# A reordered prologue: state 1 behind the second Wo piece, and five filler matmuls

## The chip, the cores and the metric

One core of one Trainium2 chip runs the kernel. The metric is the device time of one execution in microseconds (us); the median of a few runs is taken.

## The reference

There are eight batches, `x` of 8 heads x 512 x 64 and `state` of 8 heads x 32 x 64 each.

```python
def _attn_ref(x, state):
    scores = scale * x @ state^T            # softmax over the 32 states
    xread = softmax(scores) @ state         # 512 rows a head
    sread = softmax(scale * state @ x^T) @ x   # 32 rows a head
    return concatenate([xread, sread], axis=2)
def _moe_ref(x, w1, w2, w_out):             # x: 4352 tokens x 512 (8 heads x 64)
    return maximum(x @ w1, x @ w2) @ w_out  # d_ff = 1024
```

## The kernel before

The kernel folds weights together so that the large products are few. max(a, b) is written as relu(a - b) + b: `wd` = W1 - W2 (`w_sub`, L433), and W2 times Wo is folded into one 512 x 512 matrix `wwo` (`ww_mm`, L441, which reads W2 transposed by `w2_mm`, L423, and the cast Wo). For each batch `sw_mm` (L323) multiplies the batch's states by `wd` and `wwo`; `l1_mm` (L353) multiplies that by the transposed softmax `aT` and gives the hidden layer, whose relu goes to `r`; `l2_f` (L368) multiplies `r` by Wo and `l2_open` (L363) adds the `wwo` part. Batches 2 to 7 run in a loop (L550). Batches 0 and 1 run together with all the loading and preparing of weights, in a prologue whose order is written out by hand.

That order is the string `ORDER` (from L18). Each token is one step, and `step` issues the steps in sequence; each engine keeps its own in-order queue, so the order of the tokens is the order in every queue:

- A token without `:` or `>` is a DMA on SP's queue: `ldx.b.g` half of batch b's x, `ldw1.q` and `ldw2.q` a 512 KB piece of W1 or W2, `ldwo.f0.f1` a 512 KB piece of Wo, `ldS.lo.hi` the states of batches lo to hi-1, `xtd`, `atd` and `std` transposes, `store` an output.
- A token with `:` is TensorE work into the PSUM banks behind the colon: `S` transposes states (L181), `xt` x (L222), `at` the softmax (L277), `sc` the scores (L239), `sr` the state reads (L289), `w2` (L423), `ww.i.f0.f1` a part of wwo's row block i (L441), `swh.b.z` and `sw.b.4` eight row-tiled matmuls of `sw_mm` (64 rows x 32 columns of the array each, L323), `l1.b.f` two matmuls (L353), `l2p` and `l2o` parts of the second layer, `idle.n.w` n matmuls of zeros with w columns (L448), whose result nobody reads.
- A token with `>` is an eviction, a cast or other elementwise work on ScalarE (`>A`), VectorE (`>V`) or GpSimd (`>P`): `cS.lo.hi` casts states, `ce` and `cb` cast x, `cw2` and `cwo` cast weights, `sub.q.k` subtracts, `red` sums the softmax, `nm` normalises it.

State 1 means batch 1's state, 64 KB. Its steps are `ldS.1.2` (load), `cS.1.2` (cast), `S.1.2` (two transposes), `S.1.2.0` and `S.1.2.1` (two evictions), and from there `swh.1.0`, the first product with it. The second Wo piece is `ldwo.2.4`; VectorE casts it in `cwo.1`, and the first readers are `ww.3.2.4`, `ww.2.2.4` and their like. A step that writes a bank waits until what was in the bank is evicted.

Of the kernel before, what the change touches and what calls it, by code (L numbers as in the profile page):

```python
# [15 lines left out]


ORDER = """  # L18
ldx.0.1 ldx.0.0 ldw2.1 ldwo.0.2 ldS.1.2 ldw2.0 ldw1.0 ldw1.1 ldwo.2.4 ldx.1.1 ldw2.3 ldw2.2 ldwo.4.6 ldwo.6.8
ldw1.2 ldw1.3 ldx.1.0 ldx.2.1 ldx.2.0 ldS.2.8 idle.9.512:7 cS.0.1>V ce.0.2>V S.0.1:0 S.0.1.0>A ce.0.3>P xt.0.2:1  # L20
S.0.1.1>A xt.0.2>V xt.0.3:7 ce.0.0>V ce.0.1>A xt.0.3>V xt.0.0:3 xt.0.1:4 xt.0.0>A sc.0.1:5 xt.0.1>V sc.0.1>A
sc.0.0:6 cw2.1>V sc.0.0>A red.0.1>V w2.1:2 sr.0:0 w2.1>A cwo.0>P red.0.0>V cS.1.2>A sr.0>V nm.0.1>P ww.2.0.2:1
cw2.0>A S.1.2:7 ww.3.0.2:3 nm.0.0>V S.1.2.0>A w2.0:4 S.1.2.1>A sub.0.0>V at.0.0:5 w2.0>A at.0.1:6 sub.0.1>V
sub.1.1>V at.0.0>A ww.1.0.2:2 ww.0.0.2:0 at.0.1>A sub.1.0>V cwo.1>V swh.0.0:7,4 swh.1.0:5,6 swh.0.0.1>A swh.0.0.0>V
ww.1.2.4:2 swh.1.0.1>A ww.0.2.4:0 swh.1.0.0>V l1.0.0:4 l1.0.3:7 l1.0.0>A l1.0.2:6 ce.1.2>V l1.0.1:5 ce.1.3>P
l1.0.3>V l1.0.2>A xt.1.2:4 ww.2.2.4:1 l1.0.1>A xt.1.2>V cw2.3>P xt.1.3:7 ww.3.2.4:3 xt.1.3>V l2p.0.1.0.2:6 w2.3:4
cw2.2>P sc.1.1:5 w2.3>V l2p.0.3.0.2:7 sc.1.1>A l2p.0.3.2.4:7 red.1.1>V w2.2:4 l2p.0.1.2.4:6 w2.2>A l2p.0.0.0.2:5
cwo.2>V l2p.0.0.2.4:5 nm.1.1>V cwo.3>A ww.2.4.6:1 ww.0.4.6:0 ww.3.4.6:3 sub.2.1>V ww.3.6.8:3 sub.2.0>V ww.0.6.8:0
ww.3>A ww.2.6.8:1 sub.3.1>V ww.0>A ww.1.4.6:2 ww.1.6.8:2 sub.3.0>V ww.2>A l2p.0.2.0.2:4 ww.1>A ce.1.0>V swh.0.1:3,0
ce.1.1>P l2p.0.2.2.4:4 swh.0.1.1>A swh.0.1.0>V xt.1.0:1 xt.1.1:2 xt.1.0>A l1.0.5:0 xt.1.1>V cb.2.1>P l1.0.4:3  # L30
l1.0.5>A sc.1.0:1 l1.0.4>V l1.0.6:2 ce.2.3>P sc.1.0>A l1.0.7:0 ce.2.1>P l1.0.6>A red.1.0>V l2p.0.0.4.6:5
l2p.0.1.4.6:6 ce.2.2>P l1.0.7>A sw.0.4:3,1 nm.1.0>P cSm.1>A l2p.0.3.4.6:7 sw.0.4.1>V l2p.0.0.6.8:5 l2p.0.1.6.8:6
sw.0.4.0>A ce.2.0>P atd.1 l2p.0.3.6.8:7 cSm.0>A cb.2.0>P l2o.0.1:6 swh.1.2:2,0 l2.0.1>V swh.1.1:1,3 xtd.2 std
ldx.3.0 ldx.3.1 swh.1.2.0>A l2o.0.3:7 swh.1.1.0>V S.2.3:6 swh.1.2.1>A l2o.0.0:5 S2>V l2p.0.2.4.6:4 l2.0.3>A
l2.0.0>V l2p.0.2.6.8:4 swh.1.1.1>A l1.1.2:2 l1.1.3:1 l1.1.2>V l1.1.0:0 l1.1.3>A l1.1.4:6 l1.1.0>A l1.1.7:7 l1.1.1:5
l1.1.4>A l1.1.7>V l1.1.5:3 l1.1.1>A l1.1.6:2 l1.1.5>V sc.2.0:1 l1.1.6>A sc.2.1:0 l2o.0.2:4 sc.2.0>A l2.1.0:6
sc.2.1>A red.2.0>V l2.0.2>A store.0 red.2.1>V nm.2.0>P l2.1.1:7 l2.1.0>A nm.2.1>P atd.2 l2.1.1>A
"""


# [688 lines left out]
```

## Time and profile before

| | |
|---|---|
| median of 3 runs | 147.32 us (147.17 to 147.40) |
| profiled execution, its own time | 148.65 us |
| its span, first to last instruction | 146.9 us |
| TensorE busy in the span | 137.7 us (94%) |
| VectorE, ScalarE, GpSimd busy | 80.0, 70.0, 47.6 us |
| read from HBM, written | 15.20 MB, 8.91 MB |

In the profile, PE is TensorE's matmuls, PEld its weight loads, DVE VectorE, ACT ScalarE, POOL GpSimd, SP SyncE, which issues the DMAs. A timeline row gives start, length, engine, line, operation, out<-in, shape and count; what stands in brackets is the idle time of the engine before it and what ended that. The length of a row of several matmuls reaches to the modelled end of the last one, so that rows overlap a little; the pace is read from the starts.

### The profile page before, as it was taken

What the parts mean: (1) busy time and instruction counts of PE and PEld (TensorE: products, weight loads), DVE (VectorE), ACT (ScalarE), POOL (GpSimd) and SP (SyncE); (2) the same over time, 40 slices, a digit from 0 to 9 for tenths busy, and PEclk for the clock granted to TensorE, in tenths of its full rate; (3) what the DMA queues carried; (4) which work ended last, traced back from release to release, by engine and by line L of the source; (5) the groups of instructions that cost most, each with busy time, mean ns of one, the idle gap of its engine ahead of it and who ended that gap; (6) DMA issues with size and microseconds to landing.
All of it is one profiled execution on the core that took longest, in us unless ns stands there. A gap on an engine that the chain in (4) does not pass through costs nothing. (4 is left out here: it accounts for less than half of the span.)

```text
span 146.9 us, 3048 instructions
## 1 busy us (share of the span) xinstructions
PE 137.7 (94%) x1218; PEld 67.2 (46%) x1218; DVE 80.0 (54%) x159; ACT 70.0 (48%) x133; POOL 47.6 (32%) x73
## 2 busy tenths in 40 slices
PE   6857599999999999999999999999999999999991
PEld 2444156453454445444544454454445344753451
DVE  1586568764663838463854585276637485720321
ACT  4388346687782556336541835181547145510200
POOL 4233060277008806464390457056500500000000
PEclk9999999999999999999999999999999999999998
DMA  4999999932999999996989685879307032400524
GB/s 106 334 375 388 367 389 370 331 61 47 200 266 350 185 270 355 152 230 261 184 167 267 274 165 113 269 286 147 71 2 288 0 71 107 185 9 9 189 97 143
DMA packets 36979, 29.68 MB, mean 202 GB/s; under 512 B 23904, under 2 KB 32352, under 8 KB 36064
## 3 DMA queue, kind: packets, MB, share of 16 engines
q1 hardware_dynamic: 36688, 29.36, 69.7%
q8 instruction: 11, 0.18, 0.5%
q10 hardware_dynamic: 272, 0.07, 0.2%
q14 instruction: 8, 0.07, 0.2%
HBM read 15.20 MB, written 8.91 MB: 164 GB/s over the span
## 5 line engine op out<-in xcount | busy, mean ns | idle before, releaser
L368 PE MATMUL bank<-wo,r 128*128 128x512 bf16 (+2 forms) x264 | 61.5, 373 | 0.1
L368 PEld LDWEIGHTS <-r 128*128 128x128 bf16 x264 | 25.4, 98 | 29.5 <-issue 1.1
L92 ACT COPY h<-bank 128x512 f32<-128x512 f32 (+1 forms) x17 | 9.7, 573 | 48.9 <-PE bank L368 48.9
L344 DVE TENSOR_SCALAR r<-bank 128x512 bf16<-128x512 f32 x29 | 20.1, 692 | 18.6 <-PE bank L353 18.1
L353 PE MATMUL bank<-aT,sw 128*128 128x512 bf16 x128 | 29.3, 379 | 0.0
L342 ACT ACTIVATE r<-bank 128x512 bf16<-128x512 f32 x35 | 20.7, 611 | 7.2 <-PE bank L353 6.7
L255 POOL TENSOR_TENSOR a<-e,er 128x512 bf16<-128x512 bf16 x14 | 14.9, 1082 | 26.7 <-ACT e L247 16.4
L94 DVE CAST sw<-bank 128x512 bf16<-128x512 f32 x23 | 14.7, 685 | 13.1 <-PE bank L323 13.1
L96 POOL CAST xe<-h 128x512 bf16<-128x512 f32 x27 | 16.2, 634 | 16.6 <-DMA h<-in_x_dram 14.4
L363 PE MATMUL bank<-sw,aT 128*128 128x512 bf16 (+2 forms) x66 | 19.1, 374 | 0.0
L96 POOL CAST xb<-h 128x1024 bf16<-128x1024 f32 x12 | 12.3, 1042 | 19.5 <-issue 12.5
L353 PEld LDWEIGHTS <-sw 128*128 128x128 bf16 x128 | 12.1, 98 | 13.7
L94 DVE COPY h<-bank 128x512 f32<-128x512 f32 (+1 forms) x16 | 10.5, 661 | 11.8 <-PE bank L368 10.2
L92 ACT CAST sw<-bank 128x512 bf16<-128x512 f32 x25 | 13.4, 600 | 2.0 <-PE bank L323 2.0
L251 DVE TENSOR_REDUCE sums<-e 128x16 f32<-128x512 bf16 x16 | 10.6, 664 | 2.5 <-ACT e L247 2.3
L441 PE MATMUL bank<-wo,w2t 128*128 128x512 bf16 x32 | 8.0, 379 | 3.3 <-DVE wo L94 1.7
L247 ACT ACTIVATE e<-bank 128x512 bf16<-128x512 f32 x16 | 8.9, 596 | 2.4 <-PE bank L239 1.8
L363 PEld LDWEIGHTS <-aT 128*128 128x128 bf16 x66 | 5.4, 98 | 5.0 <-issue 0.7
L239 PEld LDWEIGHTS <-xt 128*128 128x128 bf16 x128 | 5.0, 98 | 2.0 <-ACT xt L92 0.3
L433 DVE TENSOR_TENSOR wd<-h,h 128x512 bf16<-128x512 f32 x8 | 5.1, 688 | 1.3 <-DMA h<-in_moe_w_dram 1.3
L441 PEld LDWEIGHTS <-w2t 128*128 128x128 bf16 x32 | 2.9, 97 | 6.2 <-issue 2.1
L239 PE MATMUL bank<-sbd,xt 128*128 128x64 bf16 x128 | 5.4, 193 | 0.2 <-ACT xt L92 0.2
(75 smaller groups left out, 99.7 us busy)
## 6 DMA issues: line engine op xcount, KB each, us to landing
...
h<-in_x_dram SPq DMA_DIRECT2D x10, 512.0 KB, 5.3
h<-in_moe_w_dram SPq DMA_DIRECT2D x8, 512.0 KB, 10.3
...
h<-in_moe_w_out_dram SPq DMA_DIRECT2D x4, 512.0 KB, 11.5
...
```

Source lines behind the costliest of these rows:

```text
L92: nc.scalar.copy(o, i)
L94: nc.vector.tensor_copy(o, i)
L96: nc.gpsimd.tensor_copy(o, i)
L239: nc.tensor.matmul(pv[:, c, kk], d["xt"][:, c, k, :], sbd[:, b, k, :], start=(c == 0 and kk == 0), stop=(c == NC - 1 and kk == 1))
L251: nc.vector.tensor_reduce(es_all[:, b, hh], e_view(b, hh), axis=AXX, op=ALU.add)
L255: (nc.gpsimd if eng == "P" else nc.vector).tensor_mul(e_view(b, hh, "a"), e_view(b, hh), d_(b)["er"][:, hh].unsqueeze(3).to_broadcast([128 ...
L342: nc.scalar.activation(out=o, in_=p, func=ACTF.Relu)
L344: nc.vector.tensor_scalar(o, p, scalar1=0.0, scalar2=None, op0=ALU.max)
L353: nc.tensor.matmul(p, SW[b][:, g, f * 128:(f + 1) * 128], AT[b][:, g].rearrange("p c t -> p (c t)"), start=(g == 0), stop=(g == 1))
L363: nc.tensor.matmul(p[:, lo:hi], AT[b][:, g, c, :], SW[b][:, g, FF + lo:FF + hi], start=(start and g == 0), stop=(stop and g == 1))
L368: nc.tensor.matmul(p[:, lo:hi], R[b][:, f, c * 128:(c + 1) * 128], wo[:, f, lo:hi], start=(start and j == 0), stop=(stop and j == len(fs) ...
L441: nc.tensor.matmul(p, w2t[:, f, i, :], wo[:, f, :], start=(f == 0), stop=(f == NF - 1))
```

## The change

Only `ORDER` changes. The set of steps is the same, but for four `idle` tokens (five matmuls) that are added; the order, the banks and the engines of many steps change.

- `ldS.1.2` moves from the fifth place of the loads, ahead of `ldw2.0`, to the place behind `ldwo.2.4`; the loads from `ldx.1.1` on keep their order.
- State 1's cast, transposes and evictions move behind `cwo.1`: `cS.1.2` stays on ScalarE, `S.1.2` stands directly ahead of `ww.3.2.4`, the evictions go from ScalarE to VectorE. `swh.1.0` moves from directly behind `swh.0.0` to between `l1.0.1` and `l1.0.3`.
- Fillers: one of 256 columns ahead of `sc.0.1`, one of 512 ahead of `xt.0.0`, two of 512 ahead of `w2.1`, one of 512 ahead of `ww.2.0.2`.
- Later in the prologue, `swh.1.2` stands alone and `swh.1.1` follows `sw.0.4` (before, `swh.1.1` followed `swh.1.2`); `cSm` (state masks) goes from ScalarE to VectorE; `std` goes behind batch 3's loads.

The diff, cut to the part that the text speaks of:

```diff
-ldx.0.1 ldx.0.0 ldw2.1 ldwo.0.2 ldS.1.2 ldw2.0 ldw1.0 ldw1.1 ldwo.2.4 ldx.1.1 ldw2.3 ldw2.2 ldwo.4.6 ldwo.6.8
+ldx.0.1 ldx.0.0 ldw2.1 ldwo.0.2 ldw2.0 ldw1.0 ldw1.1 ldwo.2.4 ldS.1.2 ldx.1.1 ldw2.3 ldw2.2 ldwo.4.6 ldwo.6.8
...
-S.0.1.1>A xt.0.2>V xt.0.3:7 ce.0.0>V ce.0.1>A xt.0.3>V xt.0.0:3 xt.0.1:4 xt.0.0>A sc.0.1:5 xt.0.1>V sc.0.1>A
-sc.0.0:6 cw2.1>V sc.0.0>A red.0.1>V w2.1:2 sr.0:0 w2.1>A cwo.0>P red.0.0>V cS.1.2>A sr.0>V nm.0.1>P ww.2.0.2:1
-cw2.0>A S.1.2:7 ww.3.0.2:3 nm.0.0>V S.1.2.0>A w2.0:4 S.1.2.1>A sub.0.0>V at.0.0:5 w2.0>A at.0.1:6 sub.0.1>V
-sub.1.1>V at.0.0>A ww.1.0.2:2 ww.0.0.2:0 at.0.1>A sub.1.0>V cwo.1>V swh.0.0:7,4 swh.1.0:5,6 swh.0.0.1>A swh.0.0.0>V
-ww.1.2.4:2 swh.1.0.1>A ww.0.2.4:0 swh.1.0.0>V l1.0.0:4 l1.0.3:7 l1.0.0>A l1.0.2:6 ce.1.2>V l1.0.1:5 ce.1.3>P
+xt.0.3:2 xt.0.2>A S.0.1.1>V xt.0.3>V ce.0.0>P idle.1.256:5 sc.0.1:6 ce.0.1>V idle.1.512:5 xt.0.0:4 sc.0.1>A xt.0.1:7 xt.0.0>V xt.0.1>A
+red.0.1>V cw2.1>P sc.0.0:3 sc.0.0>A nm.0.1>V idle.2.512:1 w2.1:5 sr.0:0 w2.1>A red.0.0>V cwo.0>P sr.0>V idle.1.512:2 ww.2.0.2:1 cw2.0>A
+nm.0.0>V ww.3.0.2:2 at.0.1:6 w2.0:4 at.0.1>A sub.0.1>V at.0.0:7 w2.0>A sub.0.0>V sub.1.0>V at.0.0>A ww.1.0.2:3
+ww.0.0.2:5 sub.1.1>V cwo.1>V swh.0.0:0,6 cS.1.2>A swh.0.0.0>A swh.0.0.1>V S.1.2:4 ww.3.2.4:2 ww.0.2.4:5 S.1.2.0>V
+S.1.2.1>V l1.0.1:7 swh.1.0:0,6 l1.0.1>V l1.0.3:4 swh.1.0.0>A ww.1.2.4:3 ce.1.3>V swh.1.0.1>A l1.0.0:7 ce.1.2>P
...
-l2p.0.1.4.6:6 ce.2.2>P l1.0.7>A sw.0.4:3,1 nm.1.0>P cSm.1>A l2p.0.3.4.6:7 sw.0.4.1>V l2p.0.0.6.8:5 l2p.0.1.6.8:6
-sw.0.4.0>A ce.2.0>P atd.1 l2p.0.3.6.8:7 cSm.0>A cb.2.0>P l2o.0.1:6 swh.1.2:2,0 l2.0.1>V swh.1.1:1,3 xtd.2 std
-ldx.3.0 ldx.3.1 swh.1.2.0>A l2o.0.3:7 swh.1.1.0>V S.2.3:6 swh.1.2.1>A l2o.0.0:5 S2>V l2p.0.2.4.6:4 l2.0.3>A
+l2p.0.2.4.6:4 ce.2.2>P l1.0.6>A swh.1.2:2,5 nm.1.0>V l2p.0.3.4.6:0 swh.1.2.0>A l2p.0.2.6.8:4 swh.1.2.1>V cb.2.0>P
+atd.1 l2p.0.3.6.8:0 cSm.0>V sw.0.4:3,1 swh.1.1:2,5 ce.2.1>P sw.0.4.0>A sw.0.4.1>V l2p.0.1.4.6:6 xtd.2 ldx.3.0
+ldx.3.1 l2p.0.1.6.8:6 swh.1.1.1>V l2o.0.1:6 l2o.0.3:0 swh.1.1.0>V l2.0.1>A l2p.0.0.6.8:7 l2.0.3>V l2o.0.0:7
...
```

More of the change, by code (lines that the diff above doesn't have):

```diff
@@ L18 @@
 ORDER = """
-ldx.0.1 ldx.0.0 ldw2.1 ldwo.0.2 ldS.1.2 ldw2.0 ldw1.0 ldw1.1 ldwo.2.4 ldx.1.1 ldw2.3 ldw2.2 ldwo.4.6 ldwo.6.8
-ldw1.2 ldw1.3 ldx.1.0 ldx.2.1 ldx.2.0 ldS.2.8 idle.9.512:7 cS.0.1>V ce.0.2>V S.0.1:0 S.0.1.0>A ce.0.3>P xt.0.2:1
-S.0.1.1>A xt.0.2>V xt.0.3:7 ce.0.0>V ce.0.1>A xt.0.3>V xt.0.0:3 xt.0.1:4 xt.0.0>A sc.0.1:5 xt.0.1>V sc.0.1>A
-sc.0.0:6 cw2.1>V sc.0.0>A red.0.1>V w2.1:2 sr.0:0 w2.1>A cwo.0>P red.0.0>V cS.1.2>A sr.0>V nm.0.1>P ww.2.0.2:1
-cw2.0>A S.1.2:7 ww.3.0.2:3 nm.0.0>V S.1.2.0>A w2.0:4 S.1.2.1>A sub.0.0>V at.0.0:5 w2.0>A at.0.1:6 sub.0.1>V
@@ L24 @@
-sub.1.1>V at.0.0>A ww.1.0.2:2 ww.0.0.2:0 at.0.1>A sub.1.0>V cwo.1>V swh.0.0:7,4 swh.1.0:5,6 swh.0.0.1>A swh.0.0.0>V
-ww.1.2.4:2 swh.1.0.1>A ww.0.2.4:0 swh.1.0.0>V l1.0.0:4 l1.0.3:7 l1.0.0>A l1.0.2:6 ce.1.2>V l1.0.1:5 ce.1.3>P
-l1.0.3>V l1.0.2>A xt.1.2:4 ww.2.2.4:1 l1.0.1>A xt.1.2>V cw2.3>P xt.1.3:7 ww.3.2.4:3 xt.1.3>V l2p.0.1.0.2:6 w2.3:4
-cw2.2>P sc.1.1:5 w2.3>V l2p.0.3.0.2:7 sc.1.1>A l2p.0.3.2.4:7 red.1.1>V w2.2:4 l2p.0.1.2.4:6 w2.2>A l2p.0.0.0.2:5
-cwo.2>V l2p.0.0.2.4:5 nm.1.1>V cwo.3>A ww.2.4.6:1 ww.0.4.6:0 ww.3.4.6:3 sub.2.1>V ww.3.6.8:3 sub.2.0>V ww.0.6.8:0
@@ L29 @@
-ww.3>A ww.2.6.8:1 sub.3.1>V ww.0>A ww.1.4.6:2 ww.1.6.8:2 sub.3.0>V ww.2>A l2p.0.2.0.2:4 ww.1>A ce.1.0>V swh.0.1:3,0
-ce.1.1>P l2p.0.2.2.4:4 swh.0.1.1>A swh.0.1.0>V xt.1.0:1 xt.1.1:2 xt.1.0>A l1.0.5:0 xt.1.1>V cb.2.1>P l1.0.4:3
-l1.0.5>A sc.1.0:1 l1.0.4>V l1.0.6:2 ce.2.3>P sc.1.0>A l1.0.7:0 ce.2.1>P l1.0.6>A red.1.0>V l2p.0.0.4.6:5
-l2p.0.1.4.6:6 ce.2.2>P l1.0.7>A sw.0.4:3,1 nm.1.0>P cSm.1>A l2p.0.3.4.6:7 sw.0.4.1>V l2p.0.0.6.8:5 l2p.0.1.6.8:6
-sw.0.4.0>A ce.2.0>P atd.1 l2p.0.3.6.8:7 cSm.0>A cb.2.0>P l2o.0.1:6 swh.1.2:2,0 l2.0.1>V swh.1.1:1,3 xtd.2 std
@@ L34 @@
-ldx.3.0 ldx.3.1 swh.1.2.0>A l2o.0.3:7 swh.1.1.0>V S.2.3:6 swh.1.2.1>A l2o.0.0:5 S2>V l2p.0.2.4.6:4 l2.0.3>A
-l2.0.0>V l2p.0.2.6.8:4 swh.1.1.1>A l1.1.2:2 l1.1.3:1 l1.1.2>V l1.1.0:0 l1.1.3>A l1.1.4:6 l1.1.0>A l1.1.7:7 l1.1.1:5
-l1.1.4>A l1.1.7>V l1.1.5:3 l1.1.1>A l1.1.6:2 l1.1.5>V sc.2.0:1 l1.1.6>A sc.2.1:0 l2o.0.2:4 sc.2.0>A l2.1.0:6
-sc.2.1>A red.2.0>V l2.0.2>A store.0 red.2.1>V nm.2.0>P l2.1.1:7 l2.1.0>A nm.2.1>P atd.2 l2.1.1>A
+ldx.0.1 ldx.0.0 ldw2.1 ldwo.0.2 ldw2.0 ldw1.0 ldw1.1 ldwo.2.4 ldS.1.2 ldx.1.1 ldw2.3 ldw2.2 ldwo.4.6 ldwo.6.8
@@ new lines @@
+ldw1.2 ldw1.3 ldx.1.0 ldx.2.1 ldx.2.0 ldS.2.8 idle.9.512:7 cS.0.1>A ce.0.2>V S.0.1:0 ce.0.3>V xt.0.2:1 S.0.1.0>V
+xt.0.3:2 xt.0.2>A S.0.1.1>V xt.0.3>V ce.0.0>P idle.1.256:5 sc.0.1:6 ce.0.1>V idle.1.512:5 xt.0.0:4 sc.0.1>A xt.0.1:7 xt.0.0>V xt.0.1>A
+red.0.1>V cw2.1>P sc.0.0:3 sc.0.0>A nm.0.1>V idle.2.512:1 w2.1:5 sr.0:0 w2.1>A red.0.0>V cwo.0>P sr.0>V idle.1.512:2 ww.2.0.2:1 cw2.0>A
+nm.0.0>V ww.3.0.2:2 at.0.1:6 w2.0:4 at.0.1>A sub.0.1>V at.0.0:7 w2.0>A sub.0.0>V sub.1.0>V at.0.0>A ww.1.0.2:3
+ww.0.0.2:5 sub.1.1>V cwo.1>V swh.0.0:0,6 cS.1.2>A swh.0.0.0>A swh.0.0.1>V S.1.2:4 ww.3.2.4:2 ww.0.2.4:5 S.1.2.0>V
@@ new lines @@
+S.1.2.1>V l1.0.1:7 swh.1.0:0,6 l1.0.1>V l1.0.3:4 swh.1.0.0>A ww.1.2.4:3 ce.1.3>V swh.1.0.1>A l1.0.0:7 ce.1.2>P
+l1.0.3>A xt.1.3:0 l1.0.0>V ww.2.2.4:1 xt.1.3>A cw2.3>P xt.1.2:6 l1.0.2:4 xt.1.2>V l2p.0.0.0.2:7 l1.0.2>V sc.1.1:0
+w2.3:6 sc.1.1>A cw2.2>V l2p.0.0.2.4:7 w2.3>A red.1.1>V l2p.0.2.0.2:4 l2p.0.2.2.4:4 cwo.2>P w2.2:0 l2p.0.1.0.2:6
+w2.2>V nm.1.1>P ww.3.4.6:2 cwo.3>A ww.2.4.6:1 ww.1.4.6:3 ww.2.6.8:1 sub.2.1>V ww.3.6.8:2 ww.2>A l2p.0.1.2.4:6
+sub.2.0>V ww.3>A ww.0.4.6:5 sub.3.0>V ww.0.6.8:5 ww.1.6.8:3 sub.3.1>V ww.0>A l2p.0.3.0.2:0 ww.1>A ce.1.1>V
@@ new lines @@
+swh.0.1:1,2 l2p.0.3.2.4:0 ce.1.0>P swh.0.1.0>A swh.0.1.1>V xt.1.1:5 xt.1.0:3 xt.1.1>A l1.0.5:1 xt.1.0>V cb.2.1>P
+l1.0.4:2 l1.0.5>A sc.1.0:5 l1.0.4>V l1.0.7:3 ce.2.3>P sc.1.0>A l1.0.6:1 ce.2.0>P l1.0.7>A red.1.0>V l2p.0.0.4.6:7
+l2p.0.2.4.6:4 ce.2.2>P l1.0.6>A swh.1.2:2,5 nm.1.0>V l2p.0.3.4.6:0 swh.1.2.0>A l2p.0.2.6.8:4 swh.1.2.1>V cb.2.0>P
+atd.1 l2p.0.3.6.8:0 cSm.0>V sw.0.4:3,1 swh.1.1:2,5 ce.2.1>P sw.0.4.0>A sw.0.4.1>V l2p.0.1.4.6:6 xtd.2 ldx.3.0
+ldx.3.1 l2p.0.1.6.8:6 swh.1.1.1>V l2o.0.1:6 l2o.0.3:0 swh.1.1.0>V l2.0.1>A l2p.0.0.6.8:7 l2.0.3>V l2o.0.0:7
@@ L38 @@
+l1.1.2:3 cSm.1>V std l2.0.0>A l1.1.1:1 l1.1.2>A l1.1.6:5 l1.1.1>V l1.1.5:2 l1.1.6>A l1.1.0:6 l1.1.5>A l1.1.3:0
+l1.1.0>V S.2.3:7 l1.1.7:3 l1.1.3>A S2>V l1.1.4:1 l1.1.7>V sc.2.1:5 l1.1.4>A sc.2.0:2 l2o.0.2:4 sc.2.0>A l2.1.1:6
+l2.0.2>A store.0 red.2.0>V sc.2.1>A nm.2.0>P red.2.1>V l2.1.0:7 l2.1.1>A nm.2.1>P atd.2 l2.1.0>A
 """
```

## The prediction

> **What bounds the kernel now.** I read the page's first two sections, then the busy time by stage, then TensorE's timeline from the last hole backwards, then the other engines and the loads at that hole.
>
> ```profile
> span 146.9 us, 3048 instructions
> PE 137.7 (94%) x1218; PEld 67.2 (46%) x1218; DVE 80.0 (54%) x159; ACT 70.0 (48%) x133; POOL 47.6 (32%) x73
> PE   6857599999999999999999999999999999999991
> PEclk9999999999999999999999999999999999999998
> ```
> ```profile
> 10.00:15.00 5.00, 3.20 (x30) 1.73 (x31) 3.63 (x8) 4.31 (x8) 2.18 (x2) 1.00 1.06 386
> 15.00:20.00 5.00, 3.31 (x29) 1.45 (x29) 3.13 (x6) 1.77 (x4) 0.88 (x2) 1.00 1.05 377
> 17.54:131.00 113.46, 113.46 (x1026) 55.01 (x1026) 68.31 (x134) 58.34 (x112) 42.64 (x53) 1.00 0.73 199
> ```
>
> In the rows by stage the columns are length, then busy time of PE, PEld, DVE, ACT and POOL, the granted clock, the DMA share and GB/s. From 17.54 to 131.00 us TensorE (PE) is busy 113.46 of 113.46 us, at a granted clock of 1.00: no other engine and no load holds it there. So the time is the moment at which this dense stretch begins, plus the TensorE work that is left behind that moment. Ahead of 17.54 TensorE has holes, and the loads run at 377 to 386 GB/s with a DMA share above 1.0. What begins the dense stretch is seen in the timelines:
>
> ```profile
> 11.20 0.27 PE L181 MATMUL bank<-ident,sb 128*128 128x128 bf16 x2
> 11.31 0.59 PE L441 MATMUL bank<-wo,w2t 128*128 128x512 bf16 x2
> 14.00 1.04 PE L441 MATMUL bank<-wo,w2t 128*128 128x512 bf16 x4 [0.66 <-ACT w2t L92]
> 14.97 0.88 PE L323 MATMUL bank<-wd,sbd 64*32 64x512 bf16 x16
> 17.54 1.02 PE L441 MATMUL bank<-wo,w2t 128*128 128x512 bf16 x4 [1.69 <-DVE wo L94]
> 18.40 1.89 PE L353 MATMUL bank<-aT,sw 128*128 128x512 bf16 x8
> ```
> ```profile
> 8.13 0.69 DVE L94 CAST w2b<-h 128x1024 bf16<-128x1024 f32 x1
> 12.61 2.58 DVE L433 TENSOR_TENSOR wd<-h,h 128x512 bf16<-128x512 f32 x4 [1.33 <-DMA h<-in_moe_w_dram]
> 16.80 0.69 DVE L94 CAST wo<-h 128x1024 bf16<-128x1024 f32 x1 [1.61 <-DMA h<-in_moe_w_out_dram]
> 17.41 1.28 DVE L94 CAST sw<-bank 128x512 bf16<-128x512 f32 x2
> ```
>
> TensorE stands still for 1.69 us until VectorE (DVE) has cast the second Wo piece (`cwo.1`), and VectorE itself waited 1.61 us for that piece to land. All earlier work on every engine is done by then. So the early part of the new order, its other choice of engines included, decides nothing as long as it is over before about 16 us.
>
> **The change part by part.**
>
> *The loads.* State 1 (64 KB) leaves its place ahead of W2's piece 0 and goes behind the second Wo piece. Its price in the old place:
>
> ```profile
> 11.18 1.05 ACT L92 CAST w2b<-h 128x1024 bf16<-128x1024 f32 x1 [0.32 <-DMA h<-in_moe_w_dram]
> ```
> ```profile
> 2.34 0.47 SPq L152 DMA_DIRECT2D h<-in_moe_w_out_dram  x1
> 2.85 0.59 SPq L156 DMA_DIRECT2D sf<-in_state_dram  x1
> h<-in_moe_w_out_dram SPq DMA_DIRECT2D x1, 512.0 KB, 7.3
> sf<-in_state_dram SPq DMA_DIRECT2D x1, 64.0 KB, 7.0
> ```
>
> At 386 GB/s a 512 KB piece takes 1.36 us. Between the cast of W2 piece 1 (8.13, which I take to follow its landing at once) and that of W2 piece 0 (11.18, started by its landing) lie 3.05 us, in which two such pieces (2.72) and state 1 came in: state 1 cost 0.33 us, about twice its bytes. It landed at 2.85 + 7.0 = 9.85, 0.2 us after the first Wo piece (2.34 + 7.3 = 9.64), and that piece came 1.5 rather than 1.36 us after the one before it: half of the 0.33 is taken from the piece in front. In the new place state 1 does the same to the second Wo piece. So W2 piece 0 and W1's pieces land 0.33 us earlier, the second Wo piece 0.33 - 0.16 = 0.17 us earlier, state 1 some 0.2 us behind it, and everything behind state 1 (x1 first) when it did before. Bounds: 0 to 0.33 us earlier.
>
> *The head of the dense stretch.* `cwo.1` then starts at 16.63 and ends at 17.32; TensorE follows 0.05 us behind, as it does now (16.80 + 0.69 = 17.49 against 17.54): 17.37. But now the two transposes of state 1 (`S.1.2`) stand in TensorE's queue directly ahead of `ww.3.2.4`, and they wait for ScalarE's cast of state 1, behind the landing:
>
> ```profile
> 10.44 0.41 ACT L92 CAST sb<-sf 128x256 bf16<-128x256 f32 x1
> 12.13 0.53 ACT L92 COPY sbd<-bank 64x128 bf16<-64x128 bf16 x2
> 15.71 1.07 ACT L92 CAST sw<-bank 128x512 bf16<-128x512 f32 x2 [0.78 <-PE bank L323]
> ```
>
> 16.63 + 0.2 + 0.41 + 0.05 = 17.29, plus 0.11 for two transposes (11.20 to 11.31) = 17.40. The two paths are nearly balanced; the dense stretch begins at 17.40 instead of 17.54: **-0.14 us**. Behind the same cast on ScalarE stands `swh.0.0.0>A` (0.57), done by 17.8, and behind `cwo.1` on VectorE `swh.0.0.1>V` (0.67), done by 17.95; their reader `l1.0.1` comes after four matmuls of `ww`, at 18.26. No stall.
>
> *The work left behind that moment.* Before the hole the old order does both `swh.0.0` and `swh.1.0` (16 row-tiled matmuls, 14.97, in a stretch that waits anyway). In the new order `swh.1.0` needs state 1, so it goes into the dense stretch, alone between `l1.0.1` and `l1.0.3`. What such a block costs there:
>
> ```profile
> 32.39 1.03 PE L368 MATMUL bank<-wo,r 128*128 128x512 bf16 x4
> 33.35 0.41 PE L323 MATMUL bank<-wwo,sbd 64*32 64x512 bf16 x8
> 33.69 1.90 PE L368 MATMUL bank<-wo,r 128*128 128x512 bf16 x8
> 35.43 0.59 PE L363 MATMUL bank<-sw,aT 128*128 128x512 bf16 x2
> 35.95 0.41 PE L323 MATMUL bank<-wwo,sbd 64*32 64x512 bf16 x8
> 36.18 0.40 PE L323 MATMUL bank<-wd,sbd 64*32 64x512 bf16 x8
> 36.51 0.60 PE L363 MATMUL bank<-sw,aT 128*128 128x512 bf16 x2
> ...
> L353 PE MATMUL bank<-aT,sw 128*128 128x512 bf16 x128 | 29.3, 379 | 0.0
> ```
>
> Eight matmuls from 33.69 to 35.43 give 0.217 us each. From 32.39 to 33.69 is 1.30 us; four of 0.217 take 0.87, so a block that stands alone costs 0.43. In the pair (35.43 to 36.51, 1.08, less 0.43) two blocks cost 0.65: the second adds only 0.22, and 0.21 is the way in and out of row tiling. The other such blocks keep their number (two alone, one pair: `swh.1.1` now follows `sw.0.4` instead of `swh.1.2`). So **+0.43 us**; bounds 0.22 and 0.43. The two state transposes cost nothing new: they fall into the wait for `cwo.1`.
>
> The Trainium skill, "TensorEngine Tiling (Array Packing)", Key Properties, says that changing the tiling mode drains TensorE, which speaks against parting the two blocks. Were each of the two changes a full drain, 0.379 (the mean length of one L353 matmul) less 0.217 apiece, the block would cost 0.54 and the sum below would be 0.11 higher; the row at 33.35 already holds both changes and gives 0.43, so the row decides.
>
> *The five fillers.* One of 256 and four of 512 columns, 0.11 + 4 x 0.217 = 0.98 us of TensorE at full clock, twice that at half. All stand ahead of `ww.2.0.2`. Their cover is the slack in front of `cwo.1`: the holes at 14.00 and 17.54 alone hold 0.66 + 1.69 us. If that cover were gone they would cost 1 us. I take nothing.
>
> *Engines.* State 1's two evictions go to VectorE (0.5, by ScalarE's 12.13 row, behind 17.95: done at 18.45; `swh.1.0` stands at 18.26 + 0.43 = 18.69), the state masks too. VectorE is busy 68.31 of 113.46 us in the dense stretch. x1's casts stay behind x1's landing:
>
> ```profile
> 18.31 0.61 POOL L96 CAST xe<-h 128x512 bf16<-128x512 f32 x1 [6.13 <-DMA h<-in_x_dram]
> ```
>
> `xt.1.3` stands eight matmuls and the block behind 18.26, at some 20.4; VectorE casts that part after `l1.0.1`'s eviction, by 20.2. Small holes here are possible, 0 to 0.2 us; I take 0. On SP, `atd.1`, `xtd.2` and x3's loads go ahead of `std`, whose result is first read in the loop at 56 us.
>
> ```profile
> 29.92 0.61 PE L222 MATMUL bank<-ident,xe 128*128 128x128 bf16 x8
> 30.42 1.04 PE L353 MATMUL bank<-aT,sw 128*128 128x512 bf16 x4
> ```
>
> *Sum:* -0.14 + 0.43 = +0.29. In the old order eight transposes of 0.055 (11.20 to 11.31 for two) take 0.44, but here 0.50 pass: a lag of 0.05 us that the new order need not repeat. Half of it off: **+0.27 us**. On the profiled execution: span 146.9 to 147.2, its own time 148.65 to 148.92. The median of the runs is 147.32, 1.33 below the profiled time; the same step gives **147.59 us**. A measurement of this kernel can tell about 0.2% (0.29 us) from no change, so the forecast is "hardly to be told from no change, on the slow side".
>
> **The rivals.**
>
> *State 1 lands late (slower).* `S.1.2` heads TensorE's queue, so whatever state 1's landing lies beyond 0.17 us behind Wo goes one for one into the time. Today's 0.2 speaks against it; for it, 256-byte packets behind a saturated queue, and x1's 512 KB directly after. If it lands half-way into x1's piece (0.7 us): 147.59 + 0.5 = 148.1. Chance 0.11.
>
> *The stretched landing goes away (faster).* From the subtraction's start (12.61, W1's piece 0 landed) to `cwo.1` (16.80) are 4.19 us for two pieces that need 2.72. A packet of another queue may explain it (queue, kind: packets, MB, share of 16 engines; the whole run, then 14.5 to 15.0 us alone):
>
> ```profile
> q8 instruction: 11, 0.18, 0.5%
> q8 instruction: 1, 0.02, 13.9%
> ```
>
> Eleven packets of 16 KB carry instructions. The one at 14.5 occupies 13.9% of 16 engines for 0.5 us, 1.1 us of one engine; I take it that it holds up that engine, and that a landing waits for the last of the 16. If the new order moves that packet behind the second Wo piece, which by bytes alone would be in at 12.61 + 2.72 - 0.17 = 15.2, the dense stretch begins 1.4 us earlier: 146.2. It decides at 0.5 us later than now. Against it: TensorE has more instructions ahead of this point, not fewer, so it asks for code earlier if at all. Chance 0.10.
> The Trainium skill, "Advanced Engine Details and Errata", ISA Cache, puts 256 instructions into a 16 KB line; by that rule the ten added loads and matmuls bring the fetch forward by up to ten instructions, on the near side, and it still holds up a landing. The trace agrees as far as it goes: 2 x 1218 TensorE instructions are 9.5 such lines.
>
> *The block costs nothing (no change, a little faster).* If `swh.1.0` falls into a hole that the new order has anyway, -0.14 alone: 147.18. Against: no hole of that kind exists now. Chance 0.08.
>
> *Row tiling drains fully (slower):* 0.11 more, 147.70. Chance 0.03.
>
> *A new hole or a lower clock (slower).* TensorE's last wait grows from 1.69 to some 2.2 us (from about 15.1 to 17.3), since `swh.1.0` left it. At its start TensorE runs at half pace, 3.81 us for nine matmuls of 512 columns, 0.42 each:
>
> ```profile
> 1.19 4.02 PE L448 MATMUL bank<-wz 128*128 128x512 bf16 x9 [1.19 <-DVE ones L453]
> 5.00 0.42 PE L181 MATMUL bank<-ident,sb 128*128 128x128 bf16 x2
> ```
>
> If a longer hole brought that pace back for 2 to 4 us of work, 1 to 2 us would be added: 148.6 to 149.6. If evictions come late in the dense stretch, 147.8 to 148. Against the first, the rows by stage show 1.00 on both sides of today's hole. Chance 0.05.
>
> **How the numbers follow.** Forecast 0.63, own range 147.35 to 147.8 (Wo's landing 0 to 0.33 earlier, the block 0.22 to 0.43, small holes up to 0.2); the bound of 147.61 cuts it, 0.36 within and 0.27 above. Faster: 0.10. Same: 0.36 + 0.08 = 0.44. Slower: 0.27 + 0.11 + 0.03 + 0.05 = 0.46. The range runs from 147.18 to 148.2: it takes in the forecast, the free block and most of the late landing, and leaves out the earlier landing and the clock.
>
> **What would show it.** In the changed profile `cwo.1` should start at 16.6, the L181 pair at 17.3 and the next L441 at 17.4; eight L323 should stand alone between two L353 rows with 0.43 us, and TensorE's busy time equal the length from there to 131. The forecast is wrong if `cwo.1` starts at 15.1 to 15.3, if L181 comes later than 17.5, or if any hole stands behind 17.5.

## The result, and the profile after

| | before | changed |
|---|---|---|
| median, lowest to highest, of 18 executions each | 147.36 us, 147.17 to 148.65 | 148.74 us, 148.12 to 151.53 |
| ratio | | 1.0094 [1.0075, 1.0114] |
| profiled execution, its own time | 148.65 us | 150.13 us |
| its span, mean granted clock | 146.9 us, 1.000 | 148.3 us, 0.988 |

The changed kernel is slower by 1.38 us, above the range of 147.18 to 148.2. Its profiled execution is one of three among the 18 (150.13, 150.19, 151.53) in which the granted clock fell; the other fifteen lie between 148.12 and 148.94. The ratios leave out executions more than 1.5% above the fastest of their kernel: here the one of 151.53 us, in the experiments two (150.38 and 150.43) of the first kernel with an fp32 warm-up.

The first two sections of the page of the changed kernel:

```profile
span 148.3 us, 3059 instructions
PE 140.2 (94%) x1223; PEld 67.9 (46%) x1223; DVE 83.6 (56%) x165; ACT 67.5 (45%) x127; POOL 47.5 (32%) x73
PE   6977599999999999999999999999999999999991
PEclk9999789999999999999999999999999999999999
```

The picture of before is still there: holes in the first five slices, then a full TensorE. The instruction counts show the edit: five more matmuls, five more weight loads, six instructions less on ScalarE and six more on VectorE. New is the clock of 7 and 8 in the fifth and sixth slices. The busy time by stage says when (columns as before):

```profile
13.08:16.49 3.41, 1.47 (x12) 0.51 (x12) 1.80 (x4) 1.22 (x2) 0.00 (x0) 1.00 1.08 357
16.49:19.90 3.41, 2.79 (x8) 0.95 (x8) 1.60 (x4) 0.89 (x2) 0.89 (x2) 0.50 1.05 386
19.90:23.30 3.40, 3.40 (x29) 1.70 (x29) 2.24 (x5) 2.16 (x4) 1.80 (x2) 1.00 1.05 387
17.30:131.00 113.70, 113.70 (x1029) 54.62 (x1028) 71.15 (x138) 56.98 (x111) 42.99 (x53) 0.99 0.75 199
```

From 17.30 to 131 TensorE is busy all the time, as predicted; but for 3.41 us, from 16.49 to 19.90, it has half its clock. TensorE's timeline of the changed kernel, then VectorE's and ScalarE's:

```profile
13.87 1.04 PE L441 MATMUL bank<-wo,w2t 128*128 128x512 bf16 x4 [0.92 <-ACT w2t L92]
14.84 0.51 PE L323 MATMUL bank<-wd,sbd 64*32 64x512 bf16 x8
17.11 0.40 PE L181 MATMUL bank<-ident,sb 128*128 128x128 bf16 x2 [1.77 <-ACT sb L92]
17.30 1.91 PE L441 MATMUL bank<-wo,w2t 128*128 128x512 bf16 x4
19.01 1.04 PE L353 MATMUL bank<-aT,sw 128*128 128x512 bf16 x2
19.98 0.41 PE L323 MATMUL bank<-wd,sbd 64*32 64x512 bf16 x8
20.32 0.60 PE L353 MATMUL bank<-aT,sw 128*128 128x512 bf16 x2
```
```profile
12.25 2.65 DVE L433 TENSOR_TENSOR wd<-h,h 128x512 bf16<-128x512 f32 x4 [0.80 <-DMA h<-in_moe_w_dram]
16.45 0.69 DVE L94 CAST wo<-h 128x1024 bf16<-128x1024 f32 x1 [1.55 <-DMA h<-in_moe_w_out_dram]
```
```profile
16.65 0.41 ACT L92 CAST sb<-sf 128x256 bf16<-128x256 f32 x1 [2.35 <-DMA sf<-in_state_dram]
```

The steps of the prediction stand here almost at their places: `cwo.1` at 16.45 (forecast 16.63), the state transposes at 17.11 (17.3), the head of the dense stretch at 17.30 (17.40), state 1's landing 0.2 us behind the second Wo piece. None of the signs that the prediction named for being wrong shows. Set against the *profiled* execution of before, and with the half clock taken off, the sum holds. What did not hold is that the profiled execution stands for the others. This is the unchanged kernel profiled once more (147.39 us, span 145.6, in the middle of its kind): TensorE (the last row has the one other wait from there to 131 us), then VectorE.

```profile
13.94 1.04 PE L441 MATMUL bank<-wo,w2t 128*128 128x512 bf16 x4 [0.66 <-ACT w2t L92]
14.91 0.89 PE L323 MATMUL bank<-wd,sbd 64*32 64x512 bf16 x16
15.95 1.02 PE L441 MATMUL bank<-wo,w2t 128*128 128x512 bf16 x4 [0.15 <-DVE wo L94]
...
20.61 0.56 PE L423 MATMUL bank<-ident,w2b 128*128 128x128 bf16 x7 [0.17 <-POOL w2b L96]
```
```profile
15.20 0.69 DVE L94 CAST wo<-h 128x1024 bf16<-128x1024 f32 x1
```

The hole of 1.69 us in front of 17.54, on which the whole prediction rested, is 0.15 us here. The second Wo piece is in by 15.2, where the prediction's rival put it "by bytes alone", and the dense stretch starts at 15.95. So in the usual execution before, as far as this profile stands for it, there is no long wait for Wo; in the changed kernel there is.

### The profile page after: what moved, and what is told of

Its sections match the earlier page's. It is cut to its first block, busy times and chain, and to the rows that moved or that the text cites. A ratio compares the mean times of both kernels' runs of the same rounds, so it can differ in the third digit from the quotient of the medians.

```text
span 148.3 us, 3059 instructions
## 1 busy us (share of the span) xinstructions
PE 140.2 (94%) x1223; PEld 67.9 (46%) x1223; DVE 83.6 (56%) x165; ACT 67.5 (45%) x127; POOL 47.5 (32%) x73
## 3 DMA queue, kind: packets, MB, share of 16 engines
HBM read 15.20 MB, written 8.91 MB: 163 GB/s over the span
## 5 line engine op out<-in xcount | busy, mean ns | idle before, releaser
L92 ACT COPY h<-bank 128x512 f32<-128x512 f32 (+1 forms) x18 | 10.3, 572 | 50.7 <-PE bank L368 45.5
L344 DVE TENSOR_SCALAR r<-bank 128x512 bf16<-128x512 f32 x31 | 21.4, 692 | 20.3 <-PE bank L353 19.7
L353 PE MATMUL bank<-aT,sw 128*128 128x512 bf16 x128 | 30.3, 383 | 0.0
L255 POOL TENSOR_TENSOR a<-e,er 128x512 bf16<-128x512 bf16 x13 | 13.4, 1049 | 31.2 <-ACT e L247 17.0
L94 DVE CAST sw<-bank 128x512 bf16<-128x512 f32 x24 | 15.3, 685 | 12.6 <-PE bank L323 12.6
L342 ACT ACTIVATE r<-bank 128x512 bf16<-128x512 f32 x33 | 19.8, 613 | 4.1 <-PE bank L353 3.7
L96 POOL CAST xe<-h 128x512 bf16<-128x512 f32 x27 | 16.3, 641 | 14.9 <-DMA h<-in_x_dram 12.7
L353 PEld LDWEIGHTS <-sw 128*128 128x128 bf16 x128 | 12.1, 98 | 13.5 <-issue 1.0
L94 DVE COPY h<-bank 128x512 f32<-128x512 f32 (+1 forms) x15 | 9.8, 661 | 10.3 <-PE bank L368 10.2
L92 ACT CAST sw<-bank 128x512 bf16<-128x512 f32 x24 | 12.8, 599 | 4.8 <-PE bank L323 4.8
L441 PE MATMUL bank<-wo,w2t 128*128 128x512 bf16 x32 | 9.0, 412 | 1.3 <-ACT w2t L92 1.3
L448 PE MATMUL bank<-wz 128*128 128x512 bf16 (+1 forms) x14 | 5.7, 534 | 1.2 <-DVE ones L453 1.2
```

What stands on the lines that cost most here:

```text
L92: nc.scalar.copy(o, i)
L94: nc.vector.tensor_copy(o, i)
L96: nc.gpsimd.tensor_copy(o, i)
L255: (nc.gpsimd if eng == "P" else nc.vector).tensor_mul(e_view(b, hh, "a"), e_view(b, hh), d_(b)["er"][:, hh].unsqueeze(3).to_broadcast([128 ...
L342: nc.scalar.activation(out=o, in_=p, func=ACTF.Relu)
L344: nc.vector.tensor_scalar(o, p, scalar1=0.0, scalar2=None, op0=ALU.max)
```

## The experiments

Three explanations were set against each other: **the instruction packet** (the five fillers put ten instructions, five weight loads and five matmuls, ahead in TensorE's stream; its next 16 KB of code comes earlier, into the second Wo piece, and holds up one of the DMA engines that carry that piece); **the order** (state 1's work inside the dense stretch costs more than reckoned); **the clock** (the wait gives half pace behind it). Each batch of four ran beside the unchanged kernel on one chip.

**The unchanged kernel, profiled again** (no edit).

> The kernel before, unchanged, profiled and timed once more. Theory A (the instruction packet decides): the profiled execution of before, 148.65, was one in which the packet held up the second Wo piece, and the usual 147.3 is the same order without it; so the new profile either shows cwo.1 near 15.3 and its own time near 147.3, or near 16.8 and 148.6. Theory B (the clock decides): cwo.1 near 16.8 in either case, and the times differ by the granted clock alone.

Measured: 147.43 us (147.22 to 148.6, ten executions), ratio 1.0002 [0.9977, 1.0026]. Its profile is the one above. In it the instruction packet comes after the Wo piece, not into it; the DMA view of 16.1 to 16.7 us (queue, kind: packets, MB, share of 16 engines):

```profile
q8 instruction: 1, 0.02, 11.7%
```

The packet begins at 16.18 us; in the profile of the prediction it began at 14.56. Of 67 executions of the unchanged kernel in these batches 8 took 148.5 to 148.7 us, as the profiled one did. That these eight were held up in the same way is likely and not shown, since none of them was profiled; three of them also had a mean clock of 0.977 to 0.988.

**The new order without the fillers.**

```diff
-idle.1.256:5
-idle.1.512:5
-idle.2.512:1
-idle.1.512:2
```

> The changed order without its five fillers (ten TensorE instructions fewer ahead of the weights). Theory A: the packet is asked for later and misses the second Wo piece as it usually does in the kernel before; 147.3 to 147.7 us. Theory B (a fall of the clock in the longer wait): the wait is as long and has less work ahead of it, so 148.7 or more, with stretches of granted clock 0.5. Theory C (the order itself is slower, fillers harmless): 148.7.

Measured: 148.31 us (147.17 to 148.96, ten), ratio 1.0042 [1.0012, 1.0072]. The packet comes at 15.53, the Wo piece lands at 14.85, the dense stretch starts at 16.22: in this profile the hold-up is gone with the fillers. But the time falls only in part, and it scatters. Two new losses show in its profile, the clock by stage and a wait of TensorE (what waited, for what: us, times, longest):

```profile
9.43:12.84 3.41, 2.65 (x43) 1.42 (x42) 2.68 (x7) 1.96 (x2) 1.11 (x1) 0.50 1.04 395
```
```profile
PE bank L353 <- DMA aT<-a: 0.4, 1, 0.4
```

Against the unchanged kernel's usual profile: head 16.22 for 15.95 (+0.27), the block +0.44, the wait for `aT` +0.43, less the one hole of 0.17 us that the unchanged kernel has behind its head: +0.97, and the spans differ by 0.9 (146.5 and 145.6). Six of the ten executions have a mean clock of 0.977 to 0.988; of the 18 with the fillers three have 0.975 to 0.989. This suggests that the fillers keep the clock up in the early holes; it does not show it.

**The old order with ten more instructions at its very start**, all in the warm-up, which ends some 10 us ahead of the wait for the second Wo piece: one 512-column matmul of zeros becomes six of 64.

```diff
-idle.9.512:7
+idle.8.512:7 idle.6.64:7
```

> The kernel before with one of its nine warm-up matmuls replaced by six of 64 columns: ten TensorE instructions more at the very start, no time added (6 x 0.053 us against 0.427), order untouched. Theory A: the packet comes as early as in the changed kernel, 148.5 to 148.8 us. Theories B and C: 147.3 us.

Measured: 148.52 us (148.26 to 148.55, four), ratio 1.0071 [1.0054, 1.0088]. TensorE's row, VectorE's, and the DMA view of 13.5 to 14.1 us:

```profile
17.40 1.02 PE L441 MATMUL bank<-wo,w2t 128*128 128x512 bf16 x4 [1.65 <-DVE wo L94]
```
```profile
16.65 0.69 DVE L94 CAST wo<-h 128x1024 bf16<-128x1024 f32 x1 [1.56 <-DMA h<-in_moe_w_out_dram]
```
```profile
q8 instruction: 1, 0.02, 11.5%
```

With nothing of the change but its count of instructions, the packet moves from 16.18 to 13.58, the Wo piece lands at 16.63, and **1.02 us** (148.52 less the 147.50 of the unchanged kernel beside it) of the 1.38 are there, without the new order and without a filler. The head moves by 1.45 us (15.95 to 17.40); 0.35 comes back behind it, of which the 0.17 us wait that the unchanged kernel has there is a part.

**The new order, no fillers, the same ten instructions at the start.**

```diff
-idle.9.512:7
+idle.8.512:7 idle.6.64:7
...
-idle.1.256:5
-idle.1.512:5
-idle.2.512:1
-idle.1.512:2
```

> The changed order without its five fillers, but with the same ten instructions added at the very start. Theory A: code position as in the changed kernel, so 148.5 to 149.0 us without any filler. Theory that the fillers themselves cost time: as the run without fillers. Theory C: 148.7.

Measured: 148.74 us (148.62 to 150.44, four), ratio 1.0127 [1.0063, 1.019]; the changed kernel's own median, though the fillers are gone. So the fillers do their harm by being counted, not by running. It gives the price of the order with the piece held up as well: 148.74 less 148.52 = **+0.22 us**. The two together are 1.24 of the 1.38 us; the rest is no more than the medians of the unchanged kernel differ from batch to batch (147.36 to 147.76). Its TensorE timeline shows the lone block at full clock:

```profile
16.97 0.28 PE L181 MATMUL bank<-ident,sb 128*128 128x128 bf16 x2 [1.64 <-ACT sb L92]
17.10 1.03 PE L441 MATMUL bank<-wo,w2t 128*128 128x512 bf16 x4
17.96 0.59 PE L353 MATMUL bank<-aT,sw 128*128 128x512 bf16 x2
18.48 0.41 PE L323 MATMUL bank<-wd,sbd 64*32 64x512 bf16 x8
18.83 0.61 PE L353 MATMUL bank<-aT,sw 128*128 128x512 bf16 x2
```

From 17.96 to 18.83 are 0.87 us; two matmuls of 0.217 take 0.43 of it, the block 0.44.

**The whole change with ten instructions taken out of the warm-up.**

```diff
-idle.9.512:7
+idle.4.512:7
```

> The changed kernel with its five fillers kept and five of the nine warm-up matmuls taken out: the code position of the weights' steps is again that of the kernel before. Theory A (the instruction packet): the packet starts at 15.2 us or later, the second Wo piece lands near 15.0, 147.3 to 147.8 us, that is 1.0 to 1.4 below the changed kernel. Theory C (the order itself costs the 1.4 us): 148.7. A shorter warm-up may leave the clock at half up to some 10 us; that part of the order has slack, so up to 0.5 more.

Measured: 148.8 us (147.91 to 148.96, ten), ratio 1.0064 [1.0037, 1.0092]: a miss by 1 us. In the profiled execution, 148.49 us, the hold-up went as foreseen (packet at 16.72, Wo piece landed at 14.94, no wait for it), yet most of the time did not. Eight of the other nine took longer than it, 148.63 to 148.96 us; whether they too were free of the hold-up is not known, since none was profiled. TensorE's timeline:

```profile
16.13 1.03 PE L441 MATMUL bank<-wo,w2t 128*128 128x512 bf16 x4
...
38.10 2.75 PE L353 MATMUL bank<-aT,sw 128*128 128x512 bf16 x12 [0.71 <-DMA aT<-a]
```

Head +0.18 against 15.95, block +0.44, wait for state 1's transposed softmax +0.71, less the hole of 0.17: +1.16; the spans differ by 1.1 (146.7 and 145.6). Taking away the first wait uncovered a second. It goes back to the transposes on SP's queue: in this run `aT` is issued at 33.71 and lands at 38.05, 4.3 us, against 33.31 to 36.66 in the unchanged kernel, 3.35 us. During it a packet of 8 KB of the other instruction queue falls at 36.68. The changed kernel has both too, but begins later, so that only some 0.07 us of it shows; its DMA view of 38.3 to 38.8 us:

```profile
q14 instruction: 1, 0.01, 10.5%
```

In the five profiles in which such a packet falls between issue and landing, `aT` takes 4.1 to 4.4 us; in the nine others 3.35 to 3.42. I take that queue to be VectorE's: its first packet in the run of the program comes when VectorE has started 62 to 66 instructions, semaphore waits counted, 64 in eleven of the fourteen profiles (so not always at the 64th, as one of the expectations below has it). The new order brings that from 43 to 45 us (unchanged order) to 36.6 to 38.3, into the transposes. State 1's evictions, moved to VectorE, do not do it alone: with them in the old order the packet comes at 44.14.

**The old order with two and with four more instructions.** These look for the edge.

```diff
-idle.9.512:7
+idle.8.512:7 idle.2.64:7
```
```diff
-idle.9.512:7
+idle.8.512:7 idle.3.64:7
```

> The kernel before, one warm-up matmul replaced by two of 64 columns: two TensorE instructions more ahead. Theory A: the kernel before stands close to the edge, since one of its profiled executions had the packet at 14.6 and another at 16.2; two instructions make the early packet more frequent, median between 147.3 and 148.6. Otherwise 147.3.

> As the last, with three matmuls of 64 columns: four TensorE instructions more ahead. Theory A: 148.5 in most executions if the packet is asked for at one fixed instruction that the sequencer passes with the group ww.1 and ww.0 (14.0 us) rather than with the group before it; otherwise 147.3 as with none.

Measured: 147.53 us (147.22 to 147.99, ten), ratio 0.9994 [0.9972, 1.0016], packet at 16.63; and 147.52 us (147.31 to 148.16, ten), ratio 0.9995 [0.9973, 1.0016], packet at 16.31. The packet is late in both profiles, and none of the 20 executions reaches 148.2 us: the first forecast, that two instructions make the early packet more frequent, missed. Somewhere between four and ten the early packet becomes the rule. The first of the two also shows a lower clock that costs nothing: half pace from 11.27 to 14.68, in front of work that waits for loads anyway, at 147.69 us.

**State 1's half alone, in the old order**: the load, cast, transposes, evictions and `swh.1.0` moved in the manner of the change (`swh.1.0` to between `l1.0.0` and `l1.0.3`), everything else as before.

```diff
-ldS.1.2 ldw2.0 ldw1.0 ldw1.1 ldwo.2.4
+ldw2.0 ldw1.0 ldw1.1 ldwo.2.4 ldS.1.2
...
-cwo.1>V swh.0.0:7,4 swh.1.0:5,6 swh.0.0.1>A swh.0.0.0>V
-ww.1.2.4:2 swh.1.0.1>A ww.0.2.4:0 swh.1.0.0>V l1.0.0:4 l1.0.3:7
+cwo.1>V swh.0.0:7,4 cS.1.2>A swh.0.0.1>A swh.0.0.0>V S.1.2:5
+ww.1.2.4:2 ww.0.2.4:0 S.1.2.0>V S.1.2.1>V l1.0.0:4 swh.1.0:5,6 swh.1.0.1>A l1.0.3:7 swh.1.0.0>V
```

> The kernel before with only the state-1 half of the change: its load behind the second Wo piece, its cast, transposes and evictions behind that, swh.1.0 alone between l1.0.0 and l1.0.3; no fillers, all else as before. Theory A: four instructions fewer ahead of the weights, the packet stays late; the forecast's own sum then shows without it: 0.14 earlier start, 0.43 for the block that stands alone, 147.5 to 147.7 us. Theory C: 148.7.

Measured: 147.72 us (147.66 to 148.56, ten), ratio 1.0009 [0.9983, 1.0036]: **+0.26 us** on the median of the unchanged kernel beside it, 147.46. The interval of the ratio takes in no change; but nine of the ten executions lie from 147.66 to 147.86, above 24 of the 31 beside them. TensorE's timeline:

```profile
15.74 0.28 PE L181 MATMUL bank<-ident,sb 128*128 128x128 bf16 x2
15.86 1.03 PE L441 MATMUL bank<-wo,w2t 128*128 128x512 bf16 x4
16.72 0.59 PE L353 MATMUL bank<-aT,sw 128*128 128x512 bf16 x2
17.25 0.41 PE L323 MATMUL bank<-wd,sbd 64*32 64x512 bf16 x8
17.59 0.60 PE L353 MATMUL bank<-aT,sw 128*128 128x512 bf16 x2
18.39 1.02 PE L353 MATMUL bank<-aT,sw 128*128 128x512 bf16 x4 [0.20 <-ACT sw L92]
```

Head -0.09, block +0.43, a hole of 0.20 behind it, less 0.17: +0.37 on the span (146.0 less 145.6 = 0.4). So state 1's half costs 0.26 us with Wo free, near the 0.22 us that the whole new order costs with Wo held up. The whole new order with Wo free was not had at that price: the run without fillers is 0.81 us above the unchanged kernel beside it (148.31 and 147.50), with a lowered clock and the wait for `aT`, and the run with ten instructions taken out 1.34 (148.80 and 147.46).

**Four attempts at a version without the hold-up**, by a warm-up with fewer instructions: eight 512-column matmuls of zeros become four of 256 columns in fp32. First the whole change with it; then also state 1's evictions and `cSm` back on ScalarE; then the old order with the five fillers and it (one of them ahead of `sc.0.0`, where the changed kernel has it ahead of `xt.0.0`); then the old order with it alone.

```diff
-idle.9.512:7
+idle4.4.256:7 idle.1.512:7
...
+    def idle4(n, w, i):
+        for j in range(n):
+            nc.tensor.matmul(banks[i][:, 0:w], wz[:, 0:256].bitcast(F32), wz[:, 0:2 * w].bitcast(F32), start=True, stop=True)
```
```diff
-S.1.2.0>V
-S.1.2.1>V
-cSm.0>V
-cSm.1>V
+S.1.2.0>A
+S.1.2.1>A
+cSm.0>A
+cSm.1>A
```

> The changed kernel with its fillers, but the nine warm-up matmuls replaced by four of 256 fp32 columns and one of 512 bf16 columns: fewer instructions at the very start, so that the weights' steps stand two instructions earlier than in the kernel before. Theory A1 (TensorE's instruction packet alone): the packet misses the second Wo piece, the dense stretch begins near 15.9, and the time is the forecast's 147.5 to 147.7. Theory A2 (a second packet, VectorE's, holds up the transpose of state 1's softmax, as in the run with five warm-up matmuls less, where the first l1.1 waited 0.7 us): 147.8 to 148.4, with a TensorE hole before l1.1.2 near 38 us. Theory C (the order itself): 148.7.

> As the last, and state 1's two evictions and the two state masks back from VectorE to ScalarE: VectorE has four instructions fewer ahead of its 64th, at which its 8 KB packet came in every profile. Theory A2: the packet comes about 2 us later, behind the transpose; no hole before l1.1.2, 147.4 to 147.7 us. Theory A1: as the last run.

> The kernel before with the same short warm-up and five fillers at the same places as in the changed kernel: fillers without a shift of the code (two instructions fewer than before). If the fillers are harmless and keep the clock up: 147.1 to 147.4 us, the spread of single runs below that of the kernel before. If they cost their own time: up to 148.4.

> The kernel before with the short warm-up alone, twelve instructions fewer ahead: the control of the last three. Theory A: no execution with the early packet, 147.2 to 147.5 us, none at 148.6. If the fp32 warm-up is too short or too long for the clock, up to 0.5 more.

The edit missed its aim. The first timeline row of the first of them:

```profile
1.19 3.78 PE L448 MATMUL bank<-wz 128*128 128x256 f32 x8 [1.19 <-DVE ones L457]
```

Four matmuls are written, eight run: the count stays what it was, and so do the packet (13.82) and the Wo piece (16.45). Measured in that order, four executions each:

| | median (lowest to highest) | ratio | packet, Wo landed |
|---|---|---|---|
| change, fp32 warm-up | 149.67 (148.15 to 150.43) | 1.0045 [0.9975, 1.0114] | 13.82, 16.45 |
| and evictions back on ScalarE | 149.32 (148.71 to 150.16) | 1.01 [1.004, 1.016] | 13.52, 16.32 |
| old order, fillers, fp32 warm-up | 148.54 (147.44 to 148.67) | 1.0027 [0.9974, 1.008] | 14.58, 15.57 |
| old order, fp32 warm-up | 147.64 (147.54 to 147.87) | 0.9985 [0.9942, 1.0028] | 16.20, 15.20 |

They say something all the same. The last shows no change from the kind of warm-up. The third, with ten instructions more again, has three of four executions at 148.49 to 148.67; its profiled one is the other, 147.44, in which the piece landed at 15.57. The second shows the other packet moving back with the evictions and masks: it comes at 40.90, and `aT` lands after 3.37 us instead of 4.1 in the changed kernel. It isn't faster for that (148.71 and 148.73 in the two executions at full clock), since behind the held-up head that wait had slack. No version here beats the kernel before.

**All fourteen profiles together** (packet begins, second Wo piece landed, us), the new order's in the second column:

| old order | new order |
|---|---|
| +10: 13.58, 16.63 | no fillers, +10 at the start: 13.47, 16.27 |
| the profile of the prediction: 14.56, 16.77 | the change: 13.78, 16.43 |
| fillers, fp32: 14.58, 15.57 | change, fp32: 13.82, 16.45 |
| again: 16.18, 15.18 | and evictions back: 13.52, 16.32 |
| fp32: 16.20, 15.20 | no fillers: 15.53, 14.85 |
| +4: 16.31, 15.19 | ten taken out: 16.72, 14.94 |
| +2: 16.63, 15.61 | |
| state 1's half: 16.34, 15.04 | |

In the six profiles in which the packet begins at 13.47 to 14.56 the piece lands at 16.3 to 16.8, in the seven in which it begins at 15.53 or later at 14.9 to 15.6. The old order with fillers, 14.58, stands 0.02 us from the first group and lands like the second, so the beginning alone does not decide.

The landings of the loads around it say more. In each of the fourteen profiles, of the 512 KB pieces that land from 9 to 24 us exactly one lands 2.4 to 3.0 us behind the landing before it, the others 1.3 to 1.7 us behind, and the packet overlaps that interval. The piece is the second Wo piece in the six held-up profiles, x1's first half in two (the run without fillers, and the old order with fillers) and W2's piece 3 in the six others; in the unchanged kernel profiled again, W2's piece 3 lands at 19.40, 2.72 us behind x1's 16.67. So in every one of these executions one load is put off. What the ten instructions at the start change is which one, and with that whether TensorE has to wait for it.

That the packet is the cause is shown as far as this goes: adding TensorE instructions alone moves both. Why the unchanged kernel's packet comes at 14.56 in one profile and at 16.18 in the other, with the same program, stays open.

## Why the prediction was wrong

**The step that failed** is the last of the sum: "The median of the runs is 147.32, 1.33 below the profiled time; the same step gives **147.59 us**." The 1.33 us were taken for a constant between a profiled execution and the timed ones. They were in the main the hold-up: it takes 1.02 us in the ten-instruction experiment, and the unchanged kernel profiled again has 147.39 in the profile and 147.43 in the median, no step at all. So the profile before already showed the wait for the second Wo piece that the change brings to the usual execution, and the sum took it to be there on both sides. The signs to watch could not catch this: all were to be read in the changed kernel's profile, and it was the profile before that was not the usual one. From the profiled time itself the sum gave 148.92; the changed kernel's median is 148.74.

**The bound** ("the time is the moment at which this dense stretch begins, plus the TensorE work that is left") held in kind, not in place. 17.54 was the head of an unusual execution; usual is 15.95, with waits of 0.66 and 0.15 in front of it.

**The loads.** W1's piece was forecast 0.33 us earlier and came 0.36 earlier (12.61 to 12.25). The second Wo piece was forecast 0.17 earlier, bounds 0 to 0.33; it came 0.34 earlier from profile to profile, 0.36 between the two held-up experiments, and between the free ones 0.14 (state 1's half alone) to 0.33 (no fillers). State 1 landed 0.2 us behind it, as forecast, and heads the queue as forecast: TensorE's wait in the changed kernel ends with ScalarE's `sb`.

**The work left behind.** The lone block: 0.43 forecast, 0.43 to 0.44 measured. That rules out the free block and the full drain (0.54); the row went before the Trainium skill's rule ("TensorEngine Tiling (Array Packing)", Key Properties), and the measurement bears the row out. The sum of +0.27 for the order was +0.22 with Wo held up; with Wo free, state 1's half alone was +0.26, and the whole order more, 0.81 and 1.34 in the two runs that had it.

**The fillers at nothing.** Their 0.98 us of TensorE were indeed covered, by 1.77 us of wait: the new order has the same 148.74 us without them, at the same count of instructions. Their price lay in what they are besides time: ten instructions in the stream, 1.02 us. And the cover that I named for them existed only because of the hold-up; usual executions have 0.15 us of it left at Wo.

**The rival of the stretched landing** had the right mechanism and the wrong sign. It explained the 4.19 us by the packet, put the free landing at 15.2 (measured 15.18), priced the difference at 1.4 us of head (1.45) and said that TensorE "asks for code earlier if at all". It did not ask whether the timed executions were held up too. Had the 1.33 us been put beside the 1.4, the case "free now, held up after" would have stood there at 147.32 + 0.27 + 1.1 to 1.4, 148.7 to 149.0. The Trainium skill's ISA Cache section ("Advanced Engine Details and Errata"), 256 instructions to 16 KB, had been read the right way round, "forward by up to ten instructions"; the runs agree that ten suffice and show that four do not.

**The rival of the clock** was real in single executions, though it does not make the median: 8 of the 30 executions of the four new-order kernels whose profile shows the held-up piece (3 of 18, 1 of 4, 2 of 4, 2 of 4) had a mean clock of 0.975 to 0.989, each at 149.9 us or more. Of the old order held up (the four of the ten-instruction experiment and, by their times, three with fillers and eight of the unchanged kernel) none took as long, though three of the eight had a lowered clock too. In the changed kernel's profile 2.6 us of work, from 17.30 to 19.90, ran at half pace and cost 1.3 us: 150.13 less that is 148.83, near the median. The wait was 1.77 us against 1.69, so its length hardly differs; the stretch before it does: 1.47 us of TensorE work in the 3.41 us before the drop, where the old order held up, with both blocks ahead of the hole, has 1.85 in 3.5.

The share of work alone does not decide, though. Five of the fourteen profiles have a drop behind the warm-up, with 1.47 to 2.18 us of TensorE work in the 3.41 us before it (2.18 in the run without fillers, 6.02 to 9.43), and two held-up profiles of the new order have no drop behind 1.60 us (no fillers, ten at the start, 13.19 to 16.60) and 1.62 us (the change with fp32 warm-up, 15.14 to 18.55, with a wait of 1.79 us in it). In all five the drop comes a whole number of 3.41 us after the clock first rose in that execution (here at 6.25; three steps later is 16.49). That rise lies anywhere from 4.1 to 8.6 us in the fourteen profiles, so the steps fall differently in each execution. What brings a drop stays open. The Trainium skill, "TensorE: Matmul & The Clock Gate", Part 1, has half rate after an idle window of some 3.4 us. The trace agrees in the length, 3.41 us of half clock, but not in the idle window: no hole of this profile was longer than 1.77 us, and the measurement decides.

**"No hole behind 17.5"** held in the changed kernel (0.07 us), but for want of an early head: in the two new-order runs without the hold-up a hole of 0.4 to 0.7 us opened at 38 us. It goes with the 8 KB packet that the new order brings into the transpose: with the evictions and masks back on ScalarE the packet comes later and `aT` lands in 3.37 us. The prediction priced their move to VectorE by VectorE's busy share alone, not by where its next code packet falls.
